# The seam between attention and experts laid out by hand: own memory for half of the split weights, earlier gathers for the first expert slot, its transposes in score banks

## The chip, the cores and the metric

The kernel runs on one core of a Trainium2 chip. The metric is the device time of one execution in microseconds (us): the median of several timed runs, and beside it one profiled execution whose trace is read here.

## What is computed

Attention with a block-causal mask feeds a two-level mixture of experts. In the reference, with 8 batches, 8 heads, 576 positions and head size 64:

```python
scores = scale * np.matmul(q, k.transpose(0, 1, 3, 2))
scores = np.where(block_i >= block_j, scores, -1e9)      # blocks of 64
attn = np.exp(scores - scores.max(-1)); attn /= attn.sum(-1) + 1e-9
x = (attn @ v).transpose(0, 2, 1, 3).reshape(4608, 512)
g_idx = argmax(x @ w_group); g_w = softmax(x @ w_group)[g_idx]          # 4 groups
e_idx = argmax(x @ w_expert[g]); e_w = softmax(...)[e_idx]              # 4 experts in each
out[tok] = g_w * e_w * (relu(x @ w1[g, e]) @ w2[g, e])                  # 512 -> 1024 -> 512
```

## The kernel before

**Attention.** The 64 heads are worked as 32 pairs, one period of the loop for each pair (`period`, about 9.4 us). A period walks the list `ORDER`, in which every word is a token with a lag: `S` scores, `D` row maximum (DVE), `E` exponential (ACT), one period later `T`/`t` transposes of the probabilities and their copies out of PSUM, two periods later `V`/`v` values and their copy. Pairs 4b to 4b+3 make batch b (0 to 7). The order of every engine's instructions is the order of the program: nothing is reordered by the scheduler. Each engine and each queue (SP's and POOL's too) takes its instructions in that order.

**Routing.** The router's tokens for batch b follow its last pair with lags of their own: `L`/`n` logits, `R` reciprocals of the sums (DVE, and a copy `rm` on POOL, L547), `Y` transposes of the logits, `M` logits times `rm` (DVE, L603) and their fold (L606 on DVE, or L608 to L610 on POOL, by `eng`), `X` rows of x to the table `xd` in HBM, `G0` to `G4` the choice of group and expert and the rank in the expert's list, `Z` the scatter of five blocks of row numbers to the table `tab` (POOL, an indirect DMA each). `early` then picks the longest list after six batches, and writes its number to `rowe`.

**Experts.** The first slot, `e`, takes 512 tokens of that longest list. SP loads its number (`index`), and fetches its row numbers (`getids`, L796, after all scatters); POOL gathers its rows (`gather`, L806 and L807). They are transposed (`xt`, L859) and split in a high and a low part (L866 on ACT, L867 on DVE). Weights arrive as `raw` and are split likewise into `wh` and `wl` (`piece`, L842 on ACT, L843 on DVE). `g1` (L891) is the first matrix product, into the two banks of `ps_s`, `g2` (L942) the second, which sums in two banks of `ps_s4` and two of `ps_t`. Once slot `e` runs, TensorE goes through 14 more slots to the end.

**PSUM.** `ps_s` has two banks, `ps_s4` one tile of two banks, `ps_t` two tags of two banks each (`psT`, taken in turn by transposes, values, logits and the rest).

**The seam.** The period of pair 31 is followed by one more (x = 32) in which only the lagged tokens are left. Then the attention's buffers are closed (`inner.close()`), `wh`, `wl` and others are opened in their place, the first weights are split, the four chunks of `e` are transposed into the four banks of `psT`, the logits of the last batch (7) follow, and then `g1` of slot `e`. The lines of ORDER to which the prediction comes back (before and after alike) are

```
Q0 X2:5 Z2:9 Z3:10 Y0:4 S0 M0:4 D8 Y1:4 V0 M1:4 v0 D7 E8 T0 ... R0:3 (word 40 of 61) ... Z1:8
```

so that in the period x = 31 batch 6 has `Y0 S0 M0 D8 Y1 V0` in this order, and its `R0` with the copy `rm` stands at word 40 of the period x = 30. Period x begins with the scores of pair x.

Of the kernel before, what the change touches and what calls it, by code (L numbers as in the profile page):

```python
# [8 lines left out]
F32 = mybir.dt.float32  # L9
F32R = mybir.dt.float32r  # L10
# [70 lines left out]
class Attention:  # L81
    def __init__(self, tc, ctx, inner, q, k, v, consts):
        self.tc, self.nc = tc, tc.nc
        self.q, self.k, self.v = q, k, v
        self.c = consts
        self.xpool = ctx.enter_context(tc.tile_pool(name="xp", bufs=2))
        self.pt = ctx.enter_context(tc.tile_pool(name="pt", bufs=2))
        self.small = ctx.enter_context(tc.tile_pool(name="small", bufs=3))
        self.ps_s = ctx.enter_context(tc.tile_pool(name="ps_s", bufs=2, space=PSUM))
        self.ps_s4 = ctx.enter_context(tc.tile_pool(name="ps_s4", bufs=1, space=PSUM))  # L90
        self.ps_t = [ctx.enter_context(tc.tile_pool(name=f"ps_t{i}", bufs=2, space=PSUM)) for i in range(2)]
        self.two = inner.enter_context(tc.tile_pool(name="two", bufs=2))
        pfix = inner.enter_context(tc.tile_pool(name="pfix", bufs=1))
        self.nat = inner.enter_context(tc.tile_pool(name="nat", bufs=3))
        vfix = inner.enter_context(tc.tile_pool(name="vfix", bufs=1))
# [152 lines left out]
        self.on_dve = on_dve  # L248
        self.scale(0, nc.vector)

    def period(self, x, N, order, hooks=(), step=7):
        hooks = list(hooks)
        if 0 <= x - 1 < N:
            self.load_v(x - 1)
        if x + 2 < N:
            self.load(x + 2)
        for n, tok in enumerate(order):
            self.token(x - lag(tok), tok, N)
            if hooks and n % step == step - 1:
                hooks.pop(0)()  # L260
        for h in hooks:
            h()

    def token(self, i, tok, N):
        if not 0 <= i < N:
# [20 lines left out]
NTB = 5  # L286
# [5 lines left out]
R = 64  # L292
# [4 lines left out]
EXEC = [0, 10, 1, 12, 2, 11, 4, 9, 3, 8, 6, 5, 7, 13]  # L297
EBAT = 6
WBUFS = 9
WARM = 14  # L300
XBUFS = 5
PIECE = 760.0
# [2 lines left out]
ILEAD = 40000.0  # L305
FREE = 7
HK = 5

TOKENS = (("G", (0, 1, 2, 4, 3)), ("X", (0, 1, 2)), ("Z", (0, 1, 2, 3, 4)))


class Router:
# [215 lines left out]
    def token(self, at, b, tok):  # L528
        nc = self.nc
        k, j = tok[0], tok[1]  # L530
# [5 lines left out]
        if k == "R":  # L536
# [3 lines left out]
            for a in range(2):  # L540
                b = 1 - a
# [34 lines left out]
        elif k == "L":  # L576
            b0, b1 = PV[j][0:2]
            n = BLK * (b1 - b0)
            ps = [at.psT(f"lg{b}_{j}_{h}") for h in range(2)]
# [98 lines left out]
    def phase4(self, at, b, st):  # L678
        nc = self.nc
        of = self.o16[b % 2].rearrange("p c g e -> p (c g e)")  # L680
        ps = at.psT(f"rk{b}")
# [49 lines left out]
class Moe:  # L731
    def __init__(self, tc, ctx, consts, ro, w1, w2, out):
        self.tc, self.nc, self.c = tc, tc.nc, consts
        self.w12 = w1, w2
        self.ro, self.out = ro, out
        self.raw = ctx.enter_context(tc.tile_pool(name="raw", bufs=4))
        self.xg = ctx.enter_context(tc.tile_pool(name="xg", bufs=XBUFS))
        self.ip = ctx.enter_context(tc.tile_pool(name="mi", bufs=5))

    def open(self, ctx):  # L740
        self.ro.late = ctx.enter_context(self.tc.tile_pool(name="late", bufs=1))
        self.wh = ctx.enter_context(self.tc.tile_pool(name="wh", bufs=WBUFS))
# [85 lines left out]
    def piece(self, s, u, z):  # L828
        nc = self.nc
        if self.direct(s, u):  # L830
            self.index(s)
            h = self.wh.tile([P, 1024], F32R, tag="wh", name=f"wh{s['n']}_{u}")
            src, n = self.wsrc(s, u)
            nc.sync.dma_start(h.bitcast(F32), src)
            s["u"][u] = (h,)
            return
        if z == 0:
            s["u"][u] = (self.wh.tile([P, 1024], F32R, tag="wh", name=f"wh{s['n']}_{u}"),
                         self.wl.tile([P, 1024], F32R, tag="wl", name=f"wl{s['n']}_{u}"))
# [7 lines left out]
        return [x.rearrange("p (c f) -> p c f", c=n) for x in s["u"][u]]  # L847

    def xt(self, s, c):
        nc = self.nc  # L850
# [4 lines left out]
        c, n = s["ch"][c]  # L855
        ps = self.at.psT(f"xp{s['n']}_{c}")
        pv = ps[:, 0:4 * n].rearrange("p (d w) -> p d w", d=4)
        for dc in range(4):
            nc.tensor.transpose(out=pv[:, dc, :], in_=s["x"][c][0:n, dc * P:(dc + 1) * P],  # L859
                                identity=self.c["ident"][0:n, 0:n])  # L860
        xh = s["xh"][:, :, c * P:c * P + n]
        xl = s["xl"][:, :, c * P:c * P + n]
        if s["small"]:
# [267 lines left out]
                self.g2(s, b)  # L1131


@with_exitstack
def attention_moe(ctx, tc, q, k, v, wcat, w1, w2, out, order=None, on_dve=None):
    nc = tc.nc
# [15 lines left out]
    with tc.manual_schedule(engines={ET.PE, ET.Activation, ET.DVE, ET.Pool, ET.SP}):  # L1152
# [11 lines left out]
        slots = [moe.slot("e", FULL, rowe, slice(0, 1))]  # L1164
        slots += [moe.slot(i, CAPS[i], rowi, slice(i, i + 1)) for i in EXEC]
        moe.plan(slots)
        for x in range(N + 1):
            hooks, step = (), 7
            if x == eb + 7:
                hooks = [lambda t=(kk, j): ro.token(at, EBAT - 1, t) for kk, js in TOKENS for j in js  # L1170
                         if (EBAT - 1, kk, j) not in ro.done]
                ear = ro.early(rowe)
                hooks += [lambda: next(ear, None)] * 3
            if x == eb + 8:
                hooks = [lambda: moe.index(slots[0]), lambda: moe.getids(slots[0]),
                         lambda: moe.pump(False), lambda: moe.gathers(0, False)]
            if 2 <= x < 8:
                hooks, step = [lambda: next(pre, None)] * HK, len(order) // HK
            at.period(x, N, order, hooks, step)
        for kk in "Vv":  # L1180
            for hf in range(2):
                at.token(N - 1, (kk, hf), N)
        for kk, js in TOKENS:
            for j in js:
                ro.token(at, NBAT - 2, (kk, j))
        inner.close()
        moe.open(ctx)
        last = NBAT - 1
        b = lambda kk, j: ro.token(at, last, (kk, j))
        fin = ro.final(rowi)  # L1190
        step = lambda: next(fin, None)
        hooks = {
            2: [lambda: b("G", 2), lambda: b("X", 2), lambda: b("X", 3)],
            3: [lambda: b("G", 4), lambda: b("G", 3)] + [lambda j=j: b("Z", j) for j in range(NTB)] + [step] * 4 + [lambda: b("X", 4), moe.hold],
            5: [lambda: moe.getids(slots[1]), lambda: moe.gathers(1e9, True)],
        }
        spl = ro.spill(at, rowo, cnti)
        for n in range(60, 66):
            hooks[n] = [lambda: next(spl, None)]
        run = moe.run(hooks)  # L1200
        moe.advance(2, 99)
        moe.xts(moe.begin[0])
        moe.advance(2, 99)
        moe.grow()
        b("R", 0)
        for j in range(2):
            b("L", j)
            b("n", 2 * j)
            b("n", 2 * j + 1)
        next(run)  # L1210
        b("X", 0)
        b("X", 1)
        for j in range(3):
            b("Y", j)
            b("M", j)
        moe.advance(2, 99)
        next(run)
        at.moe = True
        b("G", 0)
        b("G", 1)  # L1220
        for _ in run:
            pass
    moe.overflow(cnti, rowo)

# [46 lines left out]
```

## Time and profile before

| | |
|---|---|
| timed runs | median 785.43 us of 3 (785.34 to 786.76) |
| profiled execution | 783.12 us |
| its span, first to last instruction | 781.1 us |
| mean granted TensorE clock | 0.993 |
| TensorE busy | 750.5 us (96% of the span) |
| DVE, ACT, POOL busy | 512.4, 420.3, 240.7 us |

The profiled execution takes 2.0 us around its span, and lies 2.3 us below the median of the timed runs. Attention lasts to about 311 us, the experts from there to the end. [...]

### The profile page before, as it was taken

What the parts mean: (1) busy time and instruction counts of PE and PEld (TensorE: products, weight loads), DVE (VectorE), ACT (ScalarE), POOL (GpSimd) and SP (SyncE); (2) the same over time, 40 slices, a digit from 0 to 9 for tenths busy, and PEclk for the clock granted to TensorE, in tenths of its full rate; (3) what the DMA queues carried; (4) which work ended last, traced back from release to release, by engine and by line L of the source; (5) the groups of instructions that cost most, each with busy time, mean ns of one, the idle gap of its engine ahead of it and who ended that gap; (6) DMA issues with size and microseconds to landing.
All of it is one profiled execution on the core that took longest, in us unless ns stands there. A gap on an engine that the chain in (4) does not pass through costs nothing.

```text
span 781.1 us, 19675 instructions
## 1 busy us (share of the span) xinstructions
PE 750.5 (96%) x7396; PEld 600.5 (77%) x7396; DVE 512.4 (66%) x1257; ACT 420.3 (54%) x1122; POOL 240.7 (31%) x447
## 2 busy tenths in 40 slices
PE   7999999999999998799999999999999999999996
PEld 3677666767676667488998888888889888898895
DVE  4779898888888888784433534743656447555552
ACT  4887777777777774423334433533646336444541
POOL 4433262626363643322312030230332213103102
PEclk9999999999999999899999999999999999999998
DMA  4953434352525236327334483384476536637551
GB/s 162 355 177 115 152 118 156 114 180 88 181 88 181 94 116 237 117 62 299 112 111 150 159 305 152 104 285 154 142 230 229 202 118 209 251 98 250 183 169 42
DMA packets 51616, 129.80 MB, mean 166 GB/s; under 512 B 12646, under 2 KB 13286, under 8 KB 51520
## 3 DMA queue, kind: packets, MB, share of 16 engines
q1 hardware_dynamic: 42592, 103.94, 39.4%
q0 software_dynamic: 8928, 24.60, 8.8%
q8 instruction: 59, 0.97, 0.5%
q14 instruction: 37, 0.30, 0.1%
HBM read 104.05 MB, written 24.59 MB: 165 GB/s over the span
## 4 chain that ended last, share of the span: by engine, by line
PE 85%; DVE 10%; ACT 3%; issue 1%; DMA 0%; POOLq 0%; ACTq 0%
PE y L942 21%; PE h L891 20%; PE s L158 10%; PE o L228 8%; PE tp L198 6%; PE h L886 4%; DVE nm L163 3%; PE he L891 3%; PE ye L942 3%; PE y L947 2%; PE xp L859 2%; ACT pb L173 2%; DVE xns L560 2%; PE lg L583 2%; PE y L962 1%; DVE pt L203 1%
## 5 line engine op out<-in xcount | busy, mean ns | idle before, releaser
L173 ACT ACTIVATE pb<-s,nm 128x576 f32<-128x576 f32 (+8 forms) x288 | 150.3, 535 | 74.5 <-DVE nm L163 69.3
L891 PE MATMUL h<-xt,wh 128*128 128x264 f32 (+6 forms) x704 | 155.5, 312 | 0.0
L163 DVE TENSOR_REDUCE nm<-s 128x1 f32<-128x576 f32 (+8 forms) x288 | 125.1, 481 | 18.0 <-PE s L158 13.0
L891 PEld LDWEIGHTS h<-xt,wh 128*128 128x128 f32 x704 | 118.8, 188 | 8.4 <-PE y L962 1.3
L988 POOL DMA_INDIRECT out_dram<-ys,ids x40 | 41.5, 1036 | 236.7 <-DVE ys L984 219.1
L891 PE MATMUL h<-xt,wl 128*128 128x264 f32 (+6 forms) x352 | 109.2, 310 | 0.0
L942 PE MATMUL y<-wh,hring 128*128 128x512 f32 x306 | 107.2, 401 | 0.4 <-ACT ys L986 0.4
L158 PE MATMUL s<-natk,natq 64*64 64x288 f32 (+8 forms) x1280 | 101.7, 415 | 6.0 <-ACT pb L173 2.7
L228 PE MATMUL o<-pt,vb 128*64 128x64 f32 (+4 forms) x1152 | 101.0, 320 | 1.7 <-ACT pt L207 0.8
L228 PEld LDWEIGHTS o<-pt,vb 128*64 128x64 f32 x1152 | 69.6, 137 | 38.1 <-ACT pb L173 6.5
L843 DVE TENSOR_TENSOR wl<-raw,wh 128x512 fp32r<-128x512 f32 x144 | 93.0, 684 | 2.3 <-ACT wh L842 2.2
L907 ACT ACTIVATE hring<-h 128x256 fp32r<-128x256 f32 (+6 forms) x62 | 28.4, 458 | 110.1 <-PE h L891 49.6
L158 PEld LDWEIGHTS s<-natk,natq 64*64 64x64 f32 x1280 | 57.2, 132 | 37.6 <-ACT pb L173 4.3
L842 ACT CAST wh<-raw 128x512 fp32r<-128x512 f32 x144 | 82.2, 620 | 0.2
L203 DVE COPY pt<-tp 128x512 f32<-128x512 f32 x96 | 63.2, 679 | 23.9 <-PE tp L198 23.8
L914 DVE SCALAR_TENSOR_TENSOR hring<-h,hring 128x256 fp32r<-128x256 f32 (+4 forms) x85 | 33.1, 411 | 68.2 <-ACT hring L907 68.2
L198 PE MATMUL tp<-ident,pb 64*128 64x64 f32 x1536 | 67.4, 229 | 6.6 <-DVE xT L203 5.6
L129 POOL TENSOR_SCALAR natq<-natq 128x576 f32<-128x576 f32 x31 | 51.6, 1665 | 64.9 <-DMA natq<-in_q_dram 52.8
L198 PEld LDWEIGHTS tp<-ident,pb 64*128 64x128 f32 x1536 | 56.4, 138 | 13.9 <-DVE xT L203 7.4
L891 PEld LDWEIGHTS h<-xt,wl 128*128 128x128 f32 x352 | 66.1, 188 | 1.1
L942 PEld LDWEIGHTS y<-wh,hring 128*128 128x128 f32 x306 | 57.5, 188 | 12.3 <-ACT ys L986 0.6
L807 POOL DMA_INDIRECT xg<-xd,ids x40 | 40.6, 1015 | 84.2 <-PE xp L859 39.3
(221 smaller groups left out, 1164.4 us busy)
## 6 DMA issues: line engine op xcount, KB each, us to landing
raw<-in_w_dram SPq DMA_DIRECT2D x72, 512.0 KB, 4.2
vb<-in_v_dram SPq DMA_DIRECT2D x32, 384.0 KB, 4.3
natk<-in_k_dram SPq DMA_DIRECT2D x32, 288.0 KB, 4.4
natq<-in_q_dram SPq DMA_DIRECT2D x32, 288.0 KB, 4.3
wh<-in_w_dram SPq DMA_DIRECT2D x16, 512.0 KB, 6.1
xd<-xns SPq DMA_DIRECT2D x14, 512.0 KB, 3.3
keep<-in_w_dram SPq DMA_DIRECT2D x12, 512.0 KB, 4.9
kept<-in_w_dram SPq DMA_DIRECT2D x12, 512.0 KB, 6.9
```

What stands on the lines that cost most here:

```text
L129: (eng or self.nc.gpsimd).tensor_scalar(out=q, in0=q, scalar1=0.125, scalar2=None, op0=ALU.mult)
L158: nc.tensor.matmul(dst[c:c + 64], lhsT=q[ps, BLK * t:BLK * t + BLK], rhs=k[ps, k0:k0 + n], start=True, stop=True, tile_position=(64 * h, c))
L163: self.nc.vector.tensor_reduce(out=r["nm"][:, t:t + 1], in_=r["s", t], op=ALU.max, axis=AX.X if t < 8 else AX.XY, negate=True)
L173: nc.scalar.activation(reg, r.pop(("s", t)), AF.Exp, bias=r["nm"][:, t:t + 1], accum_out=self.sms[b][:, pr, t:t + 1])
L198: self.nc.tensor.transpose(out=out[a], in_=x[ps], identity=self.c["ident"][ps, ps], tile_position=(64 * a, 0))
L203: self.nc.vector.tensor_copy(dst, src)
L228: nc.tensor.matmul(o[64 * a:64 * a + 64, BLK * (t0 - b0):BLK * (t1 - b0)], lhsT=r["v"][:, a, j, :], rhs=r["pt"][:, PHALF * (a ^ f) + c0:PH ...
L842: nc.scalar.copy(h[:, sl], s["raw", u][:, sl])
L843: nc.vector.tensor_tensor(out=l[:, sl], in0=s["raw", u][:, sl], in1=h[:, sl].bitcast(F32), op=ALU.subtract)
L891: nc.tensor.matmul(o, lhsT=ww[:, dc, f], rhs=rr[:, dc, t], start=dc == 0 and x == 0, stop=dc == 3 and x == 2)
L942: nc.tensor.matmul(y[c][0:n], lhsT=hh, rhs=w, start=k == 0 and x == 0, stop=k == 7 and x == 2)
L988: i = nc.gpsimd.indirect_dma_start(out=self.out, out_offset=bass.IndirectOffsetOnAxis(ap=s["ids"][0:n, c, 0:1], axis=0), in_=ys[0:n], in_o ...
```

## The change

The two periods before the seam give up their evenly spaced hooks for hooks at given words, and the period x = 32 with all that followed it becomes one function, `seam`, with every instruction in a written order. In it:

- Five of nine `wh` buffers and four of nine `wl` buffers have memory of their own, which no attention buffer shares; the rest still lies where the attention's buffers were.
- Batch 5's scatters `Z0` to `Z3` and batch 4's `Z4` go to the period x = 29, with `early` at its end; batch 5's `Z4`, then `index`, `getids`, the first four `raw` loads and the four gathers of slot `e` go to the period x = 30 (words 2, 8 and 12), before they stood in x = 31.
- Batch 6 does the folds of `M`, `G1` and `G2` on POOL, and on DVE no more.
- The transposes of slot `e` go into the bank pair of `ps_s4` (chunks 0, 1) and the two banks of `ps_s` (chunks 2, 3); a logit tile and the rank tile of batch 6 go to `ps_s4` too. The first two weight units are split between the last attention tokens.
- Tokens of batches 6 and 7 move: batch 6's `G4`, `G3` and `Z` behind the first `g1`, batch 7's `G1`, `X0`, `X1` to the hooks behind the third step of the experts, `X2`, `X3` to those behind the fourth, `X4` behind the fifth.

```diff
     def eng(self, at, b):
-        return self.nc.vector if b >= at.nbat - 2 else self.nc.gpsimd
+        return self.nc.vector if b == at.nbat - 1 else self.nc.gpsimd
...
+        self.wpool = {("wh", 0): ctx.enter_context(tc.tile_pool(name="wh0", bufs=WHA)),
+                      ("wl", 0): ctx.enter_context(tc.tile_pool(name="wl0", bufs=WLA))}
...
+def seam(at, ro, moe, inner, ctx, N, rowi):
+    e, last, before = moe.slots[0], N // 4 - 1, N // 4 - 2
...
+    at.load_v(N - 1)
+    y, z = N - 2, N - 1
+
+    a(z, "T", 0)
+    a(z, "t", 0, 0)
+    a(z, "t", 0, 1)
+    a(y, "V", 0)
+    r(last, "R0")
+    both = at.ps_s4.tile([P, 2, 512], F32, tag="S4", name="xpe01")
+    for c in range(2):
+        moe.xt_turn(e, c, both[:, c, :])
+    a(y, "v", 0)
+    r(before, "X2")
+    moe.advance(2, 99)
+    a(y, "V", 1)
+    a(z, "T", 1)
+    a(y, "v", 1)
+    a(z, "t", 1, 0)
+    a(z, "t", 1, 1)
+    a(z, "T", 2)
+    a(z, "t", 2, 1)
+    a(z, "t", 2, 0)
+    for c in range(2, 4):
+        moe.xt_turn(e, c, at.ps_s.tile([P, 1, 512], F32, tag="S", name=f"xpe{c}")[:, 0, :])
+    moe.xt_split(e, 0)
+    moe.xt_split(e, 1)
+    a(z, "V", 0)
+    a(z, "v", 0)
+    moe.xt_split(e, 2)
+    moe.xt_split(e, 3)
+    a(z, "V", 1)
+    moe.advance(2, 99)
+    a(z, "v", 1)
+    r(before, "X1")
+    r(last, "L0", "n0", "n1", "L1", "n2", "n3")
+    r(before, "G1", "G2")
+    inner.close()
+    moe.open(ctx)
...
+    moe.hooks = {
+        2: [lambda: r(last, "G1", "G2", "X0", "X1")],
+        3: [lambda: r(last, "G4", "G3", "Z0", "Z1", "Z2", "Z3", "Z4")] + [lambda: next(fin, None)] * 4
+           + [lambda: r(last, "X2", "X3"), moe.hold],
+        4: [lambda: r(last, "X4")],
+        5: [lambda: moe.getids(moe.slots[1]), lambda: moe.gathers(1e9, True)],
+    }
+    moe.steps = moe.run(moe.hooks)
+    moe.advance(1, 99)
+    next(moe.steps)
+    r(before, "G4")
+    r(last, "Y0", "M0", "Y1", "M1")
+    r(before, "G3", "Z0", "Z1", "Z2", "Z3", "Z4")
+    next(moe.steps)
+    r(last, "Y2", "M2", "G0")
+    at.moe = True
...
-        for x in range(N + 1):
+        for x in range(N):
+            hooks = {}
+            if x == eb + 6:
+                hooks = {45 + 4 * j: [rt(EBAT - 1, "Z", j)] for j in range(4)}
+                hooks[43] = [rt(EBAT - 2, "Z", 4)]
+                hooks[60] = [lambda: next(ear, None)] * 3
             if x == eb + 7:
+                hooks = {2: [rt(EBAT - 1, "Z", 4)],
+                         8: [lambda: moe.index(e), lambda: moe.getids(e), lambda: moe.pump(False)],
+                         12: [lambda: moe.gathers(0, False)]}
```

Here `eb` is 23 and `EBAT` 6; `a` issues an attention token, `r` routing tokens of a batch.

## Rows read from the trace of the kernel before

**Rows 1.** The page's first part, busy time of TensorE.
```profile
PE 750.5 (96%) x7396; PEld 600.5 (77%) x7396; DVE 512.4 (66%) x1257; ACT 420.3 (54%) x1122; POOL 240.7 (31%) x447
```
**Rows 2.** Windows: stretch, length, busy us of each engine, granted clock, DMA share, GB/s.
```profile
301.30:319.75 18.45, 14.54 (x190) 9.71 (x190) 13.91 (x45) 8.13 (x20) 5.82 (x12) 0.91 0.43 151
319.75:334.50 14.75, 12.47 (x73) 9.92 (x67) 11.03 (x30) 3.91 (x8) 1.24 (x4) 0.88 0.46 145
...
324.10:326.60 2.50, 0.27 (x1) 0.13 (x1) 2.50 (x6) 1.43 (x3) 0.00 (x0) 1.00 0.10 26
...
316.30:319.75 3.45, 3.45 (x32) 0.72 (x32) 3.40 (x8) 1.86 (x4) 2.79 (x7) 0.51 0.50 157
326.60:330.00 3.40, 3.35 (x17) 2.76 (x18) 3.30 (x10) 0.00 (x0) 0.00 (x0) 0.50 0.91 289
```
**Rows 3.** Timeline of POOL, 271 to 302 us: start, length, instruction, idle time before.
```profile
271.03 0.32 POOL L662 TENSOR_TENSOR o<-goh,eoh 128x80 bf16<-128x80 f32 x1 [1.63 <-DVE eoh L640]
...
273.23 0.20 POOL L672 TENSOR_TENSOR gs<-gs,es 128x5 f32<-128x5 f32 x1
...
280.17 1.66 POOL L129 TENSOR_SCALAR natq<-natq 128x576 f32<-128x576 f32 x1 [6.65 <-DMA natq<-in_q_dram]
...
282.03 1.08 POOL L707 DMA_INDIRECT tab<-pay,pi  x1 [0.16 <-POOL mark L706]
...
288.43 0.90 POOL L707 DMA_INDIRECT tab<-pay,pi  x1 [0.21 <-issue]
289.33 0.23 POOL L547 COPY rm<-ri 128x40 f32<-128x40 f32 x1
...
295.43 1.09 POOL L807 DMA_INDIRECT xge<-xd,idse  x1 [5.39 <-issue]
...
300.97 1.00 POOL L807 DMA_INDIRECT xge<-xd,idse  x1 [0.27 <-POOL xge L806]
```
**Rows 4.** Timeline of SP's queue at 292 us.
```profile
292.26 0.41 SPq L796 DMA_DIRECT2D idse<-tab  x1
```
**Rows 5.** Source view of the scatter line L707, 260 to 300 us, its landing times.
```profile
DMA to landing us min/median/max: 2.0/2.1/4.5
```
**Rows 6.** Timeline, DVE and POOL: batch 5's and 6's list positions and first scatter.
```profile
278.04 0.17 DVE L701 CAST pi<-pf 128x5 int32<-128x5 f32 x1
...
312.92 0.17 DVE L701 CAST pi<-pf 128x5 int32<-128x5 f32 x1
...
313.90 1.03 POOL L707 DMA_INDIRECT tab<-pay,pi  x1 [11.75 <-DVE pi L701]
```
**Rows 7.** Timeline of DVE: M0 and the period's last copy, x = 31 and x = 27.
```profile
290.72 0.56 DVE L603 TENSOR_TENSOR tmp<-ly,rm 128x160 f32<-128x160 f32 x2
...
300.55 0.69 DVE L203 COPY pt<-tp 128x512 f32<-128x512 f32 x1
...
251.52 0.56 DVE L603 TENSOR_TENSOR tmp<-ly,rm 128x160 f32<-128x160 f32 x2
...
260.47 0.69 DVE L203 COPY pt<-tp 128x512 f32<-128x512 f32 x1 [0.43 <-PE tp L198]
```
**Rows 8.** Timeline of PE: values of pair 29, logits of batch 7.
```profile
291.10 0.88 PE L228 MATMUL o<-pt,vb 128*64 128x192 f32 x12 [0.78 <-DVE tmp L603]
...
316.27 3.56 PE L583 MATMUL lg<-xT,wcat 64*32 64x256 f32 x32 [2.99 <-DVE xte L867]
```
**Rows 9.** Groups of instructions by line, 300 to 335 us: busy us, mean ns.
```profile
L843 DVE TENSOR_TENSOR wle<-rawe,whe 128x512 fp32r<-128x512 f32 x8 | 5.1, 682 | 1.2 <-ACT whe L842 1.2
...
L606 DVE TENSOR_REDUCE lgs<-tmp 128x40 f32<-128x320 f32 (+1 forms) x3 | 1.9, 621 | 0.1
...
L603 DVE TENSOR_TENSOR tmp<-ly,rm 128x160 f32<-128x160 f32 (+1 forms) x6 | 1.5, 288 | 0.0
L914 DVE SCALAR_TENSOR_TENSOR hring<-he,hring 128x512 fp32r<-128x512 f32 x2 | 1.4, 690 | 3.3 <-ACT hring L907 3.3
```
**Rows 10.** Timeline of POOL: first gather of the second slot.
```profile
352.56 1.09 POOL L807 DMA_INDIRECT xg<-xd,ids  x1 [4.86 <-DMA ids<-tab]
```

More of the change, by code (lines that the diff above doesn't have):

```diff
@@ L249, in start, with period @@
         self.scale(0, nc.vector)
-    def period(self, x, N, order, hooks=(), step=7):
-        hooks = list(hooks)
+    def period(self, x, N, order, hooks):
         if 0 <= x - 1 < N:
@@ L258, in period @@
             self.token(x - lag(tok), tok, N)
[L259 to L262, printed above, removed]
+            for h in hooks.get(n, ()):
+                h()
     def token(self, i, tok, N):
@@ L299 @@
 WBUFS = 9
+WHA, WLA = 5, 4
 WARM = 14
@@ L578, in token @@
             n = BLK * (b1 - b0)
-            ps = [at.psT(f"lg{b}_{j}_{h}") for h in range(2)]
+            if b == at.nbat - 1 and j == 0:
+                both = at.ps_s4.tile([P, 2, 512], F32, tag="S4", name="lglast")
+                ps = [both[:, h, :] for h in range(2)]
+            else:
+                ps = [at.psT(f"lg{b}_{j}_{h}") for h in range(2)]
             for c in range(4):
@@ L680, in phase4 @@
         of = self.o16[b % 2].rearrange("p c g e -> p (c g e)")
-        ps = at.psT(f"rk{b}")
+        if b == at.nbat - 2:
+            ps = at.ps_s4.tile([P, 2, 512], F32, tag="S4", name="rkseam")[:, 0, :]
+        else:
+            ps = at.psT(f"rk{b}")
         st["rk"] = ps
@@ L749, in open, with wtile @@
         self.nring = 0
+    def wtile(self, kind, name):
+        n = self.nw[kind]
+        self.nw[kind] += 1
+        z = int(n % WBUFS >= {"wh": WHA, "wl": WLA}[kind])
+        return self.wpool[kind, z].tile([P, 1024], F32R, tag=f"{kind}{z}", name=name)
     def hold(self):
@@ L784, in getids @@
             return
+        assert all((b, "Z", j) in self.ro.done for b in range(EBAT if s["n"] == "e" else self.at.nbat) for j in range(NTB))
         self.index(s)
@@ L837, in piece @@
         if z == 0:
-            s["u"][u] = (self.wh.tile([P, 1024], F32R, tag="wh", name=f"wh{s['n']}_{u}"),
-                         self.wl.tile([P, 1024], F32R, tag="wl", name=f"wl{s['n']}_{u}"))
+            s["u"][u] = tuple(self.wtile(k, f"{k}{s['n']}_{u}") for k in ("wh", "wl"))
         h, l = s["u"][u]
@@ L849, in xt, with xt_turn, xt_split @@
     def xt(self, s, c):
+        self.xt_turn(s, c, self.at.psT(f"xp{s['n']}_{c}"))
+        self.xt_split(s, c)
+    def xt_turn(self, s, c, ps):
+        n = s["ch"][c][1]
+        pv = ps[:, 0:4 * n].rearrange("p (d w) -> p d w", d=4)
+        for dc in range(4):
+            self.nc.tensor.transpose(out=pv[:, dc, :], in_=s["x"][c][0:n, dc * P:(dc + 1) * P],
+                                     identity=self.c["ident"][0:n, 0:n])
+        s["xp", c] = pv
+    def xt_split(self, s, c):
         nc = self.nc
@@ L854, in xt @@
                                 for z in range(2)]
[L855 to L860, printed above, removed]
+        pv, n = s.pop(("xp", c)), s["ch"][c][1]
         xh = s["xh"][:, :, c * P:c * P + n]
@@ L1131, in overflow @@
                 self.g2(s, b)
+def seam(at, ro, moe, inner, ctx, N, rowi):
+    e, last, before = moe.slots[0], N // 4 - 1, N // 4 - 2
+    a = lambda i, *tok: at.token(i, tok, N)
+    r = lambda b, *toks: [ro.token(at, b, (t[0], int(t[1]))) for t in toks]
+    at.on_dve = SEAM_DVE
+    at.load_v(N - 1)
[35 more added lines that the diff above has]
+    moe.open(ctx)
+    moe.grow()
+    moe.ngat = moe.nxt = len(e["ch"])
+    fin = ro.final(rowi)
+    moe.hooks = {
[14 more added lines that the diff above has]
+    at.moe = True
 @with_exitstack
@@ L1166, in attention_moe @@
         moe.plan(slots)
-        for x in range(N + 1):
-            hooks, step = (), 7
-            if x == eb + 7:
[L1170 to L1176, printed above, removed]
-            if 2 <= x < 8:
-                hooks, step = [lambda: next(pre, None)] * HK, len(order) // HK
-            at.period(x, N, order, hooks, step)
@@ L1180, in attention_moe @@
[L1180 to L1196, printed above, removed]
+        ear = ro.early(rowe)
@@ new lines, in attention_moe @@
+        rt = lambda b, kk, j: lambda: ro.token(at, b, (kk, j))
+        e = slots[0]
+        for x in range(N):
[4 more added lines that the diff above has]
+                hooks[60] = [lambda: next(ear, None)] * 3
+            if x == eb + 7:
+                hooks = {2: [rt(EBAT - 1, "Z", 4)],
+                         8: [lambda: moe.index(e), lambda: moe.getids(e), lambda: moe.pump(False)],
+                         12: [lambda: moe.gathers(0, False)]}
+            if 2 <= x < 8:
+                step = len(order) // HK
+                hooks = {step * z + step - 1: [lambda: next(pre, None)] for z in range(HK)}
+            at.period(x, N, order, hooks)
@@ L1197, in attention_moe @@
+        seam(at, ro, moe, inner, ctx, N, rowi)
         spl = ro.spill(at, rowo, cnti)
+        hooks = moe.hooks
         for n in range(60, 66):
             hooks[n] = [lambda: next(spl, None)]
[L1200 to L1221, printed above, removed]
+        for _ in moe.steps:
             pass
```

11 lines of the change are left out of this document (6 added, 5 removed).

## The prediction

> **What bounds the kernel now.** The page's first part comes first: TensorE (PE) is busy 96% of the span [rows 1], so only its gaps, and time at the lower clock, can be won. Windows over the span put nearly all of them into one place, the seam. Between pair 30's values at 301.3 and the first product of slot `e` at 319.75 PE works 14.54 of 18.45 us, and from there to the end of the first `g2` 12.47 of 14.75 [rows 2]: 3.9 + 2.3 = 6.2 us idle. [...] The seam loses 9.6 us, and that bounds what a better seam can give. The timelines of PE, DVE and POOL then say who holds whom: the logits of batch 7 wait 2.99 us for the low part of `e`'s rows, because these hold all four banks of `psT` [rows 8].
>
> **The steps before the seam, and what they cost.** The reader should follow POOL's queue here. It takes its instructions strictly in the order written: before, the copy `rm` of batch 6 started at 289.33, the instant that the sixth scatter in front of it ended [rows 3]. The change puts `Z4` at word 2 of the period x = 30 and the four gathers at word 12, while `rm` stays at word 40. So `rm` now stands behind the gathers, these wait for their row numbers, and the row numbers wait for the last scatter to land. Step by step:
>
> - Batch 5's list positions are ready at 278.21 [rows 6]. A scatter that waited for such positions began 0.81 us after they were written (313.90 against 313.09) [rows 6], so `Z0` begins at 279.0.
> - Six scatters took 6.40 us from first start to last, 1.28 each step [rows 3]: `Z3` begins at 282.85, and ends near 283.8.
> - The scaling of pair 31's q is next in POOL's order, and the scatter behind it began 1.86 us after its start [rows 3]: `Z4` begins at 285.7. Pair 31's scores need that q only in x = 31, so its 3.6 us of delay cost nothing; if x = 31 came 3 us sooner they would.
> - The scatter lands 2.1 us later (2.0 to 4.5) [rows 5], 287.8; SP issues the fetch of the row numbers, say, 0.3 later. From that issue to the first gather it was 3.17 us [rows 3, 4]: 291.3. SP's other work behind it, the raw loads and `vb` of pair 30, has slack, as that pair's values come only in the seam.
> - Four gathers with their memsets took 6.54 us (295.43 to 301.97), and `rm` 0.23 [rows 3]: 298.05.
>
> `M0` of batch 6 on DVE reads `rm`. It began at 290.72 before [rows 7], now at 298.1, **7.4 us later**. Behind `M0` on DVE stand `D8` of pair 31 and everything after; PE stands too, since the values of pair 29 waited for that very instruction to free a bank [rows 8], and ACT waits for the row maxima. Nothing covers this. So the gathers come 4.1 us sooner, not a period, and hold up the period they were moved into. The moved `early` (about 2 us of DVE at the end of x = 29) disappears in front of this wait.
>
> Bounds: no 0.81 and 0.3 and a landing in 2.0 give 6.2; a landing in 4.5 gives 9.8. I take 7.4, because the short landing is the median.
>
> From `M0` to the period's last copy DVE needed 9.83 us (290.72 to 300.55), with three folds L606 of 1.9 us in all [rows 7, 9]. In x = 27, where POOL folds, it needed 8.95 (251.52 to 260.47) [rows 7]. Moving batch 6's folds to POOL so gives 0.9 back; a gain of 0 to 1.9 is possible.
>
> After some 7 us of idle PE the clock will be at 0.5, as after both waits of [rows 2], for some 3.4 us again, which loses up to 1.7. The period's PE work has over a microsecond of room inside DVE's 8.95, so I take 0.4 (0 to 1.7). [...]
>
> The seam so begins 7.4 - 0.9 + 0.4 = **6.9 us later** (5.3 to 10.6).
>
> **The seam itself.** Own buffers let ACT and DVE split units 0 and 1 between attention's tokens, in which no store has to land first. The score banks free `psT`, so that the wait of 2.99 us [rows 8] goes. What is late next? I list PE's and DVE's work in the written order, in the times of before.
>
> PE: 14.54 us to the first product, of which 1.7 were lost to the clock [rows 2]; without these and the rank sums, some 12.4. The transposes `T0` of pair 31 now fill the hole ahead of pair 30's values. The first product so starts near 314 instead of 319.75. After it come rank sums, `Y0`, `Y1`, the second product, `Y2`, and PE is free for the first `g2` near 321.
>
> DVE: 13.9 us of busy time lay in that stretch [rows 2]. Batch 6's folds and normalizers leave, about 1.6. In front of the rank's reader there are added: the wait for POOL's `G2`, 2.4 us from 271.03 to 273.43 [rows 3] and 0.2 for its start; unit 2's two splits, 1.4; the low part of h, 0.7; `M0` and `M1` of batch 7, 2.6 [rows 9]; and the rest of `R0`, about 1 by estimate. That is 20.6 us without a gap, 301.3 to 321.9, and about 322.8 with 1 us of gaps. The first `g2` needs the bank pair of `ps_s4`, which holds the rank tile until `G3` has read it on DVE: PE waits 1.8 to 1.9 us there, a wait that the change puts in. With 0.5 for small ones PE keeps 2.4 of 9.6 us, and the seam wins **7.2 us**. Bounds: all 9.6; or 4.5, if DVE is a microsecond later still and the wait lowers the clock (1.7), for which the wait ahead of 326.6, with 0.27 us of work in 2.50 [rows 2], is the nearest row.
>
> **Behind the seam.** Batch 7's tokens come in another order, but DVE has the same work before the second slot's list: `G1`, `X0`, `X1` move behind the first `g2`, `X2` and `X3` behind `final`. I cost this at nothing, since `final`'s end comes at the same place to within a microsecond, and the gather at 352.56 waits for its row numbers [rows 10]; the late stores of `X2` to `X4` could take up to 1.5 us if that cover is gone. Own memory, `load_v` and `hold` cost no engine time.
>
> **Sum.** 783.12 + 6.9 - 7.2 = 782.8 for the profiled execution. The timed median lies 2.3 higher: **785.1 us**. 0.2% is 1.6 us, about what a measurement of this kernel can tell from no change.
>
> **The rivals.**
>
> *The gathers don't hold up M0.* Then the row numbers would have to be there near 283; the seam's 7.2 and the folds' 0.9 remain, 777.3 us. For it: DVE had `early` in the way at 290 before. Against it: POOL's order [rows 3], and that five scatters can't be through before 285. Chance 0.10.
>
> *The hold-up at its lower bound, the seam at its best.* With 5.3 and 9.6 the time is 781.1; halfway, 782 or so. It needs PE without a wait for the rank tile. Chance 0.10.
>
> [...] Chance 0.18, with a fall of the clock at the rank tile in it.
>
> *The forecast,* a hold-up that the seam pays back, 0.62: 782 to 788 by itself.
>
> **How the numbers follow.** Faster by over 0.2%: both fast rivals, 0.20, and 0.16 of the forecast's lower side, 0.36. Slower: 0.18 and 0.10 of its upper side, 0.28. Within: 0.36. The range runs from 779.5 to 789.5: below it lies the first rival, above it the worst of the third.
>
> **What would show each step.** In the changed kernel's timeline of POOL: `rm` of batch 6 right behind the fourth `xge` gather, at 297 to 300; on DVE `M0` just behind it; on PE an idle stretch of 6 to 8 us there, and a clock near 0.5 after it. In the seam: no wait of the logits for `xte`, the first product some 14 us behind the period's last copy, and the first `ye` waiting for DVE's `base`. I am wrong if `rm` lies near 289, if PE has no hole at 290 to 298, or if the seam wins less than 4 us.

## The result: 0.64% slower

| | before | after |
|---|---|---|
| timed runs | median 784.84 us of 6 (783.04 to 786.76) | median 789.66 us of 6 (789.15 to 790.55) |
| profiled execution | 783.12 us | 790.52 us |
| span, mean granted clock | 781.1 us, 0.993 | 788.8 us, 0.987 |

The ratio of the two is 1.0064, with an interval of 1.0047 to 1.008, some 5.0 us. I had forecast 785.1 us and at most 789.5. The two profiled executions stand 7.4 us apart, more than the medians, as the one lies below its median and the other above. They have 1.4 us between them ahead of anything that the change touches. Timelines of PE, the scores of pair 28, the first line of before and the second of after:

```profile
264.44 1.95 PE L158 MATMUL s<-natk,natq 64*64 64x320 f32 x28
265.84 1.95 PE L159 MATMUL s<-natk,natq 64*64 64x320 f32 x28
```

The same scores of an early period start at 25.05 and 26.47, so the 1.4 us are there from the start on. They aren't of the change: e1, which is the same program up to the seam's end, has the early ones at 25.04, and of the eleven runs below only e3 starts as late as after (26.45). I call this the early 1.4 and take it off where I compare starting times.

First POOL's queue, the lines that answer to [rows 3]: timeline of POOL after, with start, length, instruction and the idle time ahead of it.

```profile
279.89 0.99 POOL L711 DMA_INDIRECT tab<-pay,pi  x1 [3.32 <-DVE pi L705]
...
286.65 0.96 POOL L711 DMA_INDIRECT tab<-pay,pi  x1 [0.20 <-issue]
287.61 0.54 POOL L820 MEMSET xge<- 128x512 f32 x1
291.65 1.08 POOL L821 DMA_INDIRECT xge<-xd,idse  x1 [3.50 <-issue]
...
297.19 1.00 POOL L821 DMA_INDIRECT xge<-xd,idse  x1 [0.27 <-POOL xge L820]
298.19 0.23 POOL L544 COPY rm<-ri 128x40 f32<-128x40 f32 x1
```

`rm` starts at the instant at which the fourth gather ends, and three engines (DVE, PE and ACT) stand until then, before their next work idle for 6.95, 5.96 and 7.51 us. Timeline of DVE after (for [rows 7]):

```profile
298.45 0.55 DVE L604 TENSOR_TENSOR tmp<-ly,rm 128x160 f32<-128x160 f32 x2 [6.95 <-POOL rm L544]
...
308.73 0.69 DVE L204 COPY pt<-tp 128x512 f32<-128x512 f32 x1 [0.42 <-PE tp L199]
```

Timeline of PE after (for [rows 8]), from the hold-up to the fourth product of slot `e`:

```profile
298.83 1.55 PE L229 MATMUL o<-pt,vb 128*64 128x192 f32 x12 [5.96 <-DVE tmp L604]
...
320.82 0.74 PE L911 MATMUL he<-xte,whe 128*128 128x512 f32 x2
...
330.57 0.47 PE L962 MATMUL ye<-whe,hring 128*128 128x512 f32 x1 [2.03 <-DVE t L703]
...
335.78 0.71 PE L911 MATMUL he<-xte,whe 128*128 128x512 f32 x2
...
340.68 0.63 PE L566 MATMUL xn<-ident,xT 128*128 128x128 f32 x4 [1.23 <-DVE t L703]
...
343.66 0.39 PE L962 MATMUL ye<-whe,hring 128*128 128x512 f32 x1
347.58 0.63 PE L566 MATMUL xn<-ident,xT 128*64 128x128 f32 x4 [3.53 <-DVE xns L569]
347.97 0.82 PE L911 MATMUL he<-xte,whe 128*128 128x512 f32 x2
```

Four waits stand here, and none of the long ones of [rows 8]. The first two were forecast: the hold-up at 298.83, and the rank tile at 330.57. The last two were not: the transposes of `X3` wait 1.23 us for a bank that the second rank tile holds, and those of `X4` 3.53 us for a bank that DVE empties late. Windows after (columns as in [rows 2]) show what lies behind each wait:

```profile
298.83:304.00 5.17, 5.17 (x60) 4.07 (x64) 3.71 (x8) 2.57 (x6) 2.24 (x6) 0.50 0.28 107
...
331.00:335.00 4.00, 4.00 (x13) 3.05 (x12) 3.57 (x16) 0.62 (x3) 2.71 (x5) 0.57 0.04 10
...
335.78:347.97 12.19, 7.43 (x46) 5.70 (x44) 10.89 (x54) 1.68 (x4) 7.22 (x14) 1.00 0.30 90
...
348.50:351.60 3.10, 3.10 (x9) 2.33 (x8) 1.42 (x3) 0.00 (x0) 0.00 (x0) 0.50 0.61 207
```

The kernel before did the step from third to fourth product without a gap, and at the full clock (1.00); its window:

```profile
335.14:341.61 6.47, 6.47 (x37) 5.14 (x36) 5.26 (x27) 1.77 (x4) 0.30 (x1) 1.00 0.21 81
```

Put together, the 7.4 us of the two profiles are, in us and rounded (a "product" is the `g1` of one step of slot `e`):

| stretch | before | after | difference |
|---|---|---|---|
| up to the scores of pair 28 | 264.44 | 265.84 | +1.4 |
| from there to the period's last copy | 36.11 | 42.89 | +6.8 |
| last copy to first product | 19.20 | 12.09 | -7.1 |
| first to third product | 15.39 | 14.96 | -0.4 |
| third to fourth product | 6.47 | 12.19 | +5.7 |
| fourth product to slot 1 | 30.27 | 31.79 | +1.5 |
| rest | | | -0.5 |

So the hold-up and the seam cancel, nearly as forecast, and the loss lies behind the seam, where I had forecast nothing: 7.2 us in these two executions. Not all of the 7.2 is waiting. From third to fourth product PE is busy for 7.43 us after and for 6.47 before: the transposes of `X2` and `X3`, some 0.8 us, stood ahead of the third product before and stand behind it now. The waits in that step are 12.19 - 7.43 = 4.8 us, and the 1.5 behind it is the half clock of the last window (0.50 for 3.10 us). DVE's timeline after says whom `X4` waits for:

```profile
340.99 0.17 DVE L705 CAST pi<-pf 128x5 int32<-128x5 f32 x1
341.07 0.17 DVE L406 TENSOR_TENSOR fin<-base,eb 64x16 f32<-64x16 f32 x1
...
346.77 0.15 DVE L406 TENSOR_TENSOR fin<-fin,fin 64x1 int32<-64x1 f32 x1
346.85 1.27 DVE L569 TENSOR_TENSOR xns<-xn,ri 128x512 f32<-128x512 f32 x2
```

`final`, the choice of the other slots once batch 7 is routed, is some 40 small instructions on DVE, 5.8 us in a row. The change puts `X2` and `X3` in the program behind them, so the two instructions that empty their banks start at 346.85. Once attention is over `psT` hands out one tag of two banks, and both are held by `X2` and `X3`; `X4`, and behind it on PE the fourth product, stand until 347.58.

### The profile page after: what moved, and what is told of

Its sections match the earlier page's. It is cut to its first block, busy times and chain, and to the rows that moved or that the text cites. A ratio compares the mean times of both kernels' runs of the same rounds, so it can differ in the third digit from the quotient of the medians.

```text
span 788.8 us, 19683 instructions
## 1 busy us (share of the span) xinstructions
PE 753.3 (96%) x7396; PEld 603.0 (76%) x7396; DVE 508.6 (64%) x1243; ACT 420.0 (53%) x1124; POOL 245.1 (31%) x468
## 4 chain that ended last, share of the span: by engine, by line
PE 57%; DVE 2%; issue 1%; POOL 1%; ACT 1%; DMA 0%; POOLq 0%
PE y L962 21%; PE h L911 20%; PE h L906 4%; PE ye L962 3%; PE y L967 2%; PE xp L870 2%; PE he L911 2%; PE y L982 1%; PE o L229 1%; POOL xge L821 1%; DMA xd<-xns 0%; PE tp L199 0%; PE s L159 0%; DVE wle L856 0%; POOL xge L820 0%
## 5 line engine op out<-in xcount | busy, mean ns | idle before, releaser
L159 PE MATMUL s<-natk,natq 64*64 64x288 f32 (+8 forms) x1280 | 104.2, 424 | 5.2 <-ACT pb L174 2.7
```

The source lines that it names most:

```text
L159: nc.tensor.matmul(dst[c:c + 64], lhsT=q[ps, BLK * t:BLK * t + BLK], rhs=k[ps, k0:k0 + n], start=True, stop=True, tile_position=(64 * h, c))
```

## The experiments

Each ratio is to the kernel before on the same chip, with its 95% interval; "after" has 1.0064. Runs on different chips are compared by ratio, as the chips differ: the kernel before took 784.48, 794.1 and 784.4 us (medians of 21, 17 and 17) on the three chips of e1 to e4, e5 to e8 and e9 to e11.

| label | what it is | median us | ratio |
|---|---|---|---|
| e1_x23_first | after, `X2`, `X3` ahead of `final` | 783.62 | 0.9998 [0.9987, 1.0009] |
| e2_rm_first | after, gathers behind `rm` | 785.12 | 1.0008 [0.9997, 1.0019] |
| e3_both | both of these | 780.57 | 0.9949 [0.9934, 0.9964] |
| e4_hooks_alone | before, early hooks | 791.86 | 1.0103 [1.0086, 1.0121] |
| e5_split_gathers | e1, gathers two and two | 786.76 | 0.9906 [0.9885, 0.9926] |
| e6_rank_first | e5, rank tile read early | 787.86 | 0.9915 [0.9894, 0.9935] |
| e7_folds_on_dve | e3, batch 6's folds on DVE | 787.12 | 0.9921 [0.9902, 0.994] |
| e8_own_memory_alone | before, own buffers | 792.16 | 0.9979 [0.9962, 0.9995] |
| e9_x3_later | e6, `X3` with `X4` | 773.95 | 0.9862 [0.9841, 0.9884] |
| e10_g2_on_dve | e9, `G1`, `G2` of batch 6 on DVE | 772.74 | 0.9849 [0.9827, 0.987] |
| e11_score_banks_alone | before, score banks | 783.93 | 1.0 [0.9982, 1.0018] |

My theory was that the loss is the order around `final`, against three rivals: the hold-up alone costs more than its trace shows; the fall of the clock in the seam does it; a part of the change that I took as a gain is a loss. The first four runs take the two suspects away, singly and together, and put the hold-up alone into the kernel before.

**e1_x23_first.**

```diff
-           + [lambda: next(fin, None)] * 4
-           + [lambda: r(last, "X2", "X3"), moe.hold],
+           + [lambda: r(last, "X2", "X3")]
+           + [lambda: next(fin, None)] * 4 + [moe.hold],
```

> The changed kernel with one move: the rows X2 and X3 of the last batch go ahead of the four steps of the final choice instead of behind them. Theory A (the loss behind the seam is a wait for a bank: X4's transposes wait 3.5 us until DVE has emptied X2's bank, which it does only after the final choice, and the clock falls for it): the 3.5 us of idle PE at 344 to 347.6 and the low clock behind them go, 5 us are won, 784 to 785.5 us. Rival (the final choice comes 1.3 us later and the second slot's rows with it, so that PE waits there instead): 788 us or more, with a wait of PE or POOL at the second slot's transposes.

It wins 0.66% on the change (1.0064 to 0.9998), some 5.2 us, with nothing but two tokens moved past `final`. Timelines of its DVE and PE:

```profile
338.91 0.17 DVE L705 CAST pi<-pf 128x5 int32<-128x5 f32 x1
338.99 1.28 DVE L569 TENSOR_TENSOR xns<-xn,ri 128x512 f32<-128x512 f32 x2
340.19 0.16 DVE L406 TENSOR_TENSOR fin<-base,eb 64x16 f32<-64x16 f32 x1
```

```profile
338.60 0.63 PE L566 MATMUL xn<-ident,xT 128*128 128x128 f32 x4 [1.24 <-DVE t L703]
...
341.83 0.60 PE L566 MATMUL xn<-ident,xT 128*64 128x128 f32 x4
```

`xns` now comes ahead of `fin`, `X4` doesn't wait, and the clock is 1.00 from 340 to 350. The traces give the same price: the third to the fourth product takes 8.48 us (12.19 after), and from there to slot 1 it is 30.18 us (31.79 after, 30.27 before), together 5.3. `X3`'s wait is still there with 1.24 us; no run takes it alone out of this kernel, so its price is read from the trace. The step behind the seam then costs 5.2 + 1.2 = 6.4 us, and with the 0.8 us of transposes that moved into it this is the 7.2 of the table. It is more than the whole loss of the change. In e1 the clock still falls behind the first `ye` (0.50 from 329 to 331), so the fall of the clock in the seam, the second rival, doesn't carry this loss.

**e2_rm_first.**

```diff
-                         12: [lambda: moe.gathers(0, False)]}
+                         41: [lambda: moe.gathers(0, False)]}
```

> The changed kernel with one move: the four gathers of the first slot go from word 12 to word 41 of their period, behind the copy rm of batch 6. Theory A (the gathers hold up rm and through it M0 and everything): rm is back at about 290, the 6 us of idle PE at 293 to 299 go, 5 to 7 us are won, 783 to 785 us. Rival 1 (POOL's folds of batch 6 now wait behind the gathers, and the third M, which takes the first one's buffer, waits for them on DVE): 2 to 3 us of the gain are lost, 786 to 787 us. Rival 2 (the hold-up was hidden and is absorbed elsewhere): no gain, 789 to 790 us.

It wins 0.56%, 4.4 us, on the change. `rm` is at 288.64 in its timeline of POOL, so `M0` is held up no more, but then the folds of batch 6, which the change moved to POOL, stand behind the gathers:

```profile
288.64 0.22 POOL L544 COPY rm<-ri 128x40 f32<-128x40 f32 x1 [2.77 <-DVE ri L541]
...
289.86 1.08 POOL L821 DMA_INDIRECT xge<-xd,idse  x1 [0.54 <-POOL xge L820]
...
296.43 0.53 POOL L609 TENSOR_TENSOR tmp<-tmp 128x160 f32<-128x160 f32 x1
```

DVE's `M2` then waits 2.45 us for the fold, and PE's next values 2.25 for `M2`, as rival 1 had it, though the time lies at the edge of theory A. The hold-up is not gone; some 2.3 us are left of it, and a stretch at the clock of 0.50 (299 to 302).

**e3_both.**

> Both moves: gathers behind rm, and X2 and X3 ahead of the final choice. Theory A (two separate waits, whose prices add): 10 to 12 us below the changed kernel, 778 to 780 us, 5 to 6 us below the kernel before. If the two hide each other the gain is that of one, 784 us.

1.15% under the change, 9.1 us; the single prices were 5.2 and 4.4, so they add within the intervals, though the time lies just above the 778 to 780 expected. What is left are the wait behind the folds (2.29 us), the rank tile (2.04) and `X3` (1.59).

**e4_hooks_alone.** The kernel before, with the change's hooks in x = 29 and x = 30 and nothing else of it (the part for x = 30):

```diff
...
+            if x == eb + 7:
+                hk = {2: [rt(EBAT - 1, "Z", 4)],
+                      8: [lambda: moe.index(slots[0]), lambda: moe.getids(slots[0]), lambda: moe.pump(False)],
+                      12: [lambda: moe.gathers(0, False)]}
```

> The kernel before with the early hooks alone: scatters of batch 5 in the period before, row numbers and gathers at words 8 and 12 of x = 30, all else as before. Theory A: M0 of batch 6 starts at 298 instead of 291 and the seam behind it is no shorter than before: 790 to 793 us, 6 to 7 us slower than before. Rival 2 (absorbed, since the first slot's rows come 4 us sooner and DVE has caught up by the seam): within 1.5 us of the kernel before.

1.03% slower, 8.1 us. Waits on DVE and PE, and the seam's old wait:

```profile
296.52 0.56 DVE L605 TENSOR_TENSOR tmp<-ly,rm 128x160 f32<-128x160 f32 x2 [6.97 <-POOL rm L549]
...
308.58 0.69 DVE L203 COPY pt<-tp 128x512 f32<-128x512 f32 x1
```

```profile
296.89 1.55 PE L228 MATMUL o<-pt,vb 128*64 128x192 f32 x12 [5.98 <-DVE tmp L605]
...
324.32 3.16 PE L585 MATMUL lg<-xT,wcat 64*32 64x256 f32 x32 [3.01 <-DVE xte L869]
```

Windows of e4 show how long the clock stays low behind that wait:

```profile
304.00:305.00 1.00, 1.00 (x15) 0.51 (x8) 0.22 (x1) 0.69 (x3) 0.00 (x0) 0.51 0.00 0
305.00:306.00 1.00, 1.00 (x24) 0.81 (x24) 0.77 (x4) 0.79 (x4) 0.00 (x0) 1.00 0.00 0
```

It is near 0.50 from 296.9 to 305, and from `M0` to the period's last copy it takes 12.06 us (9.83 before, 10.28 after). So the hold-up by itself does cost more than the 6.8 us of the table, as the first rival had it, but this is not the loss behind the seam, which e1 takes away with the hold-up in place. Earlier gathers alone win nothing: what the logits wait for in the seam isn't the rows of `e` but the banks, and these waits stay as they were.

**e8_own_memory_alone and e11_score_banks_alone**, the two other parts by themselves on the kernel before. e8 gives it the pools `wh0` and `wl0` and nothing of the new order; e11 takes the transposes' banks from the scores:

```diff
-        ps = self.at.psT(f"xp{s['n']}_{c}")
+        if s["n"] == "e" and c < 2:
+            if c == 0:
+                self.xpe01 = self.at.ps_s4.tile([P, 2, 512], F32, tag="S4", name="xpe01")
+            ps = self.xpe01[:, c, :]
+        elif s["n"] == "e":
+            ps = self.at.ps_s.tile([P, 1, 512], F32, tag="S", name=f"xpe{c}")[:, 0, :]
```

> The kernel before with nothing but the own memory for five wh and four wl buffers. Before, the first weight split waited 2.41 us for a store to land, because its buffer lay where the stored rows had lain. Theory: the wait goes, the rows' low parts on DVE come 1.1 us sooner, and with them the logits and the first product: 1 to 1.5 us won, 783 to 783.5 us. Rival (another wait ends there): no gain.

> The kernel before with nothing but the four chunks of the first slot's transposes in the score banks. Before, the logits of batch 7 waited 2.99 us, since the four chunks held all banks of psT until DVE had split them. Theory: the logits run at once behind the transposes, the first product is then bound by the last split (end near 318) instead of the logits' end (319.75): 1.5 to 2 us won. Rival (the wait only moves ahead of the first product, and the clock falls there): within 0.7 us of the kernel before.

e8 wins 0.21%, some 1.7 us: the wait of the logits falls from 2.99 [rows 8] to 1.68 us. e11 wins nothing. The logits wait no more, but the transposes do (timeline of PE):

```profile
311.10 0.64 PE L866 MATMUL xpe<-ident,xge 128*128 128x128 f32 x4
316.04 2.82 PE L866 MATMUL xpe<-ident,xge 128*128 128x128 f32 x12 [4.31 <-DVE xte L874]
```

In the order of before, a chunk is split right behind its transposes. Chunk 1 goes into the same pair tile as chunk 0 and stands until DVE has split that one. The seam's order issues all transposes of a tile ahead of its splits, and after has neither wait; that the banks pay only together with that order follows from this, but no run has the order without the banks. Neither part is a loss by itself, which answers the third rival as far as these two go.

**e5_split_gathers, e6_rank_first, e7_folds_on_dve** try what is left in e3. e5 is e1 with the gathers in two halves, each where POOL has room; e6 is e5 and reads the rank tile before `Y0`, `M0`, `Y1`, `M1` of batch 7; e7 is e3 with `eng` as it was before. The diff has the gathers of e5 first, and behind the dots what e6 adds.

```diff
-                         12: [lambda: moe.gathers(0, False)]}
+                         41: [lambda: [moe.gather(e, c) for c in (0, 1)]]}
+            if x == eb + 8:
+                hooks = {33: [lambda: [moe.gather(e, c) for c in (2, 3)]]}
...
-    r(before, "G4")
+    r(before, "G4", "G3")
     r(last, "Y0", "M0", "Y1", "M1")
-    r(before, "G3", "Z0", "Z1", "Z2", "Z3", "Z4")
+    r(before, "Z0", "Z1", "Z2", "Z3", "Z4")
```

> The changed kernel with X2 and X3 ahead of the final choice, and the gathers cut in two: chunks 0 and 1 behind rm (word 41 of x = 30), chunks 2 and 3 behind the third fold of batch 6 (word 33 of x = 31). Theory A (with all four gathers behind rm, DVE still waits 2.45 us for POOL's first fold behind them, and PE's clock falls for the 2.3 us that it idles): 2.5 to 4 us below the 780.6 us of the version with four gathers behind rm, 776.5 to 778 us. Rival (the late chunks 2 and 3 hold up the transposes, or DVE is the bound of that period whatever POOL does): 780 to 781 us.

> As the version with the gathers cut in two, and G3 of batch 6 goes ahead of Y0, M0, Y1, M1 of batch 7. Theory A (the first second product waits 2.0 us for the bank pair that holds batch 6's rank tile until DVE reads it): that wait shrinks by 1 to 2 us, 775.5 to 777 us. Rival (Y2 or the last two banks of the product wait instead, since M0 and M1 free theirs 1.2 us later): no gain, within 0.7 us of the version with the gathers cut in two.

> The version with all four gathers behind rm and X2, X3 ahead of the final choice, and batch 6's folds and normalizers back on DVE. Theory A (what is left there is the wait of 2.45 us for POOL's folds behind the gathers, and in the seam 2.5 us for POOL's G2): both waits go, DVE takes on 1.9 us of folds and 1.5 us of G2, 1.5 to 3 us below 780.6 us. Rival (DVE is the bound of that period, and more work on it costs what the wait cost): 780 to 782 us.

e5 lies 0.43% under e3, and its PE has no wait for the folds. e7 lies 0.28% under e3: with folds that don't queue behind gathers the hold-up goes too, by another way. These are differences between chips, hardly wider than the intervals, and those of e5 and e7 overlap: which way is better stays open. e6 is a miss. Its first `ye` starts without the wait of 2.04 us, yet it is no faster. The timeline of its PE shows the wait handed on:

```profile
326.40 0.56 PE L199 MATMUL ly<-ident,lt 64*128 64x64 f32 x4 [1.21 <-DVE tmp L604]
...
334.72 0.20 PE L688 MATMUL rk<-o,tri 128*128 128x96 bf16 x1 [0.64 <-DVE xns L569]
...
337.57 1.09 PE L566 MATMUL xn<-ident,xT 128*128 128x128 f32 x4 [1.59 <-DVE t L703]
```

`Y2` waits 1.21 us for a bank instead, as the rival had it. PE comes to `X3` sooner, but DVE has as much to do before it as ever, and behind that wait the clock falls: 0.57 on average from 336 to 344.

**e9_x3_later and e10_g2_on_dve.** So `X3` has to go to where its bank is free: behind the second rank tile's reader and the next `ye`, beside `X4`. e10 moves batch 6's `G1` and `G2` back to DVE, with its `M` folds still on POOL.

```diff
-        3: [lambda: r(last, "G4", "G3", "Z0", "Z1", "Z2", "Z3", "Z4")] + [lambda: next(fin, None)] * 4
-           + [lambda: r(last, "X2", "X3"), moe.hold],
-        4: [lambda: r(last, "X4")],
+        3: [lambda: r(last, "G4", "G3", "Z0", "Z1", "Z2", "Z3", "Z4"), lambda: r(last, "X2")]
+           + [lambda: next(fin, None)] * 4 + [moe.hold],
+        4: [lambda: r(last, "X3", "X4")],
```

> The version with the gathers cut in two and G3 of batch 6 ahead of M0, and X3 goes one step further, with X4 behind the fifth step, so that only X2 stands ahead of the final choice. Theory A (in that version X3's transposes wait 1.6 us for the bank that holds batch 7's rank tile, and the clock falls behind it, which ate what the earlier rank of batch 6 had won): both go, ratio to the kernel before 0.987 to 0.989, where the version without this move had 0.9915. Rival (DVE is a step behind anyway, and the wait moves to the next bank): 0.991 to 0.992.

> As the version with X3 later, and batch 6's G1 and G2 run on DVE (its folds of M stay on POOL). Theory A (DVE stands still for 2.5 us until POOL's G2 is done, and DVE's own G2 takes 1.5): the first second product starts about 1 us sooner, ratio 0.001 lower than with X3 later alone. Rival (PE no longer waits there, or waits for M0's banks): no difference.

e9 wins 1.38% on the kernel before (10.8 us), e10 1.51% (11.8 us, and 17 us by ratio on the change). e9 and e6 ran on different chips, but their traces agree with the ratios (0.9915 to 0.9862, some 4.2 us): from the third product to slot 1 e6 takes 43.00 us and e9 39.38, so `X3`'s wait of 1.59 us and the clock behind it cost 3.6. The intervals of e9 and e10 overlap, but the two ran on one chip, and all four times of e10 (772.61 to 772.90) lie below all four of e9 (773.41 to 774.42): 1.2 us, near the 0.001 expected. e9's wait of 1.17 us at `Y2`, ahead of the first `ye`, is gone in e10. The page's first part and windows of e10 show what became of the seam:

```profile
PE 746.6 (97%) x7396; PEld 599.5 (78%) x7396; DVE 510.1 (66%) x1252; ACT 419.9 (54%) x1124; POOL 242.4 (31%) x456
```

```profile
310.00:320.00 10.00, 9.42 (x93) 6.76 (x88) 9.36 (x33) 4.04 (x11) 0.70 (x1) 1.00 0.43 143
320.00:330.00 10.00, 8.81 (x49) 6.85 (x48) 9.15 (x34) 3.10 (x7) 4.72 (x11) 1.00 0.22 74
330.00:340.00 10.00, 10.00 (x50) 8.20 (x49) 9.40 (x45) 1.62 (x3) 5.14 (x9) 1.00 0.26 93
```

PE is busy for 3.9 us less than before [rows 1], with as many instructions: none of its seam runs at the half clock (1.00 in the windows from 300 to 340). DVE is busy for 9 us and more of each 10, and the chain of work that ended last lies almost wholly on DVE from 309.6 to 327.7 and on PE behind that: up to 327.7 DVE, not PE, is now the tight engine.

## Why the prediction was wrong

**The step that failed** is "Behind the seam": "I cost this at nothing, since `final`'s end comes at the same place to within a microsecond", with 1.5 us as its bound. It cost 6.4 us (5.2 for the order against `final` by e1, 1.2 for `X3` by its wait in the traces); the 7.2 of the table has the moved transposes besides. I counted DVE's work, which is the same in either order, and asked whether `final` and the list would come late; they didn't. I did not ask who holds which bank meanwhile. The walk that I had done for the rank tile ahead of the first `ye`, applied to `psT`, shows the wait: the two tokens that empty its banks stand behind 5.8 us of `final`, and PE has 3 us of `ye` to do meanwhile (341.06 to 344.05). Of the 6.4 us I had zero; had I had them, the sum would have been 782.8 + 6.4 = 789.2 for a profile, and 791.5 for the median by the 2.3 us of then, against 790.52 (1.4 of it early) and 789.66 measured. The 2.3 did not hold: the profile after lies 0.9 above its median.

**The hold-up** was right in its place and its mechanism. `rm` was forecast to end at 298.05 and ends at 298.42, `M0` was forecast at 298.1 and lies at 298.45; but the early 1.4 taken off, `M0` is 6.3 us later instead of 7.4. The first scatter starts 0.3 us behind the list positions and not 0.8, and from `Z4`'s start to the first gather it takes 5.0 us and not 5.6; the four gathers take 6.54, as forecast. The terms behind `M0` were off the other way: from there to the last copy it took 10.28 us, 0.45 more than before, where I had 0.9 less for the folds and 0.4 more for the clock. The half clock lasted from 298.83 to 304.0, 5.2 us instead of 3.4. The sum of it, 6.8 us, was forecast as 6.9, and that it is so near is luck: one part was 1.1 too long, the other 1.0 too short. My bounds of 5.3 to 10.6 also left out that I had allowed the folds 0 to 1.9; with it they are 4.3 to 11.5. POOL's queue kept the written order: `rm` starts at 298.19 behind four gathers, while in e2, without them ahead of it, its input let it start at 288.64.

**The seam** won 7.1 us to the first product and 0.4 to the third, 7.5 of a forecast 7.2, with the wait at the first `ye` of 2.03 us (forecast 1.8 to 1.9). Of the 7.5 some 0.8 are the transposes that moved behind the third product, so 6.7 were won. The first product lies 12.1 us behind the last copy, not the 14 that I had in mind, but the half clock behind the `ye` wait gave 1.6 us back (the first second product, from its first `ye` to the transposes behind it, takes 4.42 us, 2.80 before). Of the 9.6 us that I had as its loss, 3.4 were my estimate that the work of the two stretches at 0.51 and 0.50 [rows 2] takes half as long at 1.00, and no run shows that term. What the runs show are the second product of `e`, 4.20 us before (327.51 to 331.71, at 0.50 up to 330.0) and 3.03 after at 1.00 (324.73 to 327.76), and the logits, which start 3.48 us ahead of the first product before and 1.13 after; before, their second half also waited 0.87 us for ACT's copy of the first. By e4 the seam seems worth more: the hold-up costs 8.1 us by itself, the step behind the seam 6.4, and the change 5.0 in all, which leaves 9.5 for the seam if the three add. But in e4 DVE still folds, the clock stays low longer (8.1 us against 5.2), and the stretch from `M0` to the last copy takes 1.8 us more than after; without these the seam is left 7.7. The 1.0 us between 6.7 and 7.7 stays open.

**The rivals.** A half clock through the whole period of pair 31, the slower case to which I gave 0.18, did not happen: the clock was back at 304.0, 4.7 us ahead of the last copy. That case held the right sign for a wrong reason, so it is luck that the measured time lies on its side. The nearest to it is e4, with the half clock for 8 us. The first rival, gathers that don't hold up `M0`, was made true in e2: with the tokens where the change puts them the gathers then hold up the folds, and only with the split in e5, or with the folds on DVE in e7, is there no hold-up left.

## What to carry to other kernels

Before a reader of PSUM is moved, list for each bank the writer who comes next, and what the emptying instruction now stands behind on its engine: equal work on that engine says nothing about when the bank comes free (`X4` stood 3.53 us for one). It was so with a queue here: the gathers, moved forward to be early, delayed what they were put in front of, and a 0.2 us copy behind the four, which wait for their row numbers and then take 6.5 us, cost 8 us in e4. When a large rearrangement gives little, look for a gain and a loss of equal size; here moving one line in each of two places gave 9 us back.

## What the runs showed of the hardware

In these runs the clock's fall does not go by the length of the wait alone. The first `ye` waits 2.03 us after and 2.04 in each of e1, e2, e3 and e5, behind the same instructions. After, the clock is 0.50 from 332 to 334; in e1 it is 0.50 from 329 to 331, in e2 from 326 to 329, in e5 from 331 to 333; in e3 the windows read 1.00 up to 342. Nor does the longer wait always do it: `X3` waits 2.50 us in e7 and the clock stays at 1.00 up to 350, while it falls behind the 1.59 us (with two short gaps ahead) in e6, to 0.50 from 338 to 342. PE in e7, and the window behind its wait:

```profile
340.12 0.63 PE L566 MATMUL xn<-ident,xT 128*128 128x128 f32 x4 [2.50 <-DVE t L703]
...
341.00:342.00 1.00, 1.00 (x6) 0.79 (x6) 0.96 (x4) 0.00 (x0) 0.63 (x1) 1.00 0.38 152
```

Windows of e3, the wait and the stretch behind it:

```profile
324.20:326.30 2.10, 0.07 (x3) 0.03 (x1) 2.03 (x7) 0.00 (x0) 0.00 (x0) 1.00 0.81 236
...
327.00:328.00 1.00, 1.00 (x6) 0.78 (x5) 0.96 (x4) 0.00 (x0) 0.41 (x1) 1.00 0.00 0
328.00:329.00 1.00, 1.00 (x6) 0.83 (x5) 0.86 (x5) 0.22 (x1) 0.79 (x2) 1.00 0.07 16
```

What else decides it, none of these runs tests. For a forecast, a wait of 2 us on PE costs here, by my estimate, either 2.0 or about 3.7 (2.03, and with it the 1.6 above).

On the second chip, e6 runs the same program as e9 up to the gap at `X3`, and yet its DVE is busy for 0.69 us between 280 and 285 where that of e9 is busy for 4.59. Timeline of DVE in e6:

```profile
279.35 0.55 DVE L164 TENSOR_REDUCE nm<-s 128x1 f32<-128x384 f32 x1
283.33 0.69 DVE L204 COPY pt<-tp 128x512 f32<-128x512 f32 x1 [3.43 <-PE s L159]
285.64 0.49 DVE L204 COPY lt<-lg 128x320 f32<-128x320 f32 x1 [1.61 <-remote]
```

e8 shows a like hole at 285 to 290 (DVE busy for 0.69 us), and e5 and e7 have waits of 3.40 and 3.05 us on DVE in the same period. The kernel before was not profiled on that chip, though it too was 10 us slower there. What the engines waited for, the records don't show, and I leave it open; the ratios of e5 to e8 may hold some of it.
